# The sums of w34 begin in batch 0, in five operations for seven

## The chip, the cores and the metric

The kernel runs on one core of a Trainium2 chip. The metric is the device time of one execution in microseconds (us). Three runs of the kernel before took 485.19, 485.21 and 486.02 us, with a median of 485.21 us. The engines are TensorE (PE in the profile, PEld for its weight loads), VectorE (DVE), ScalarE (ACT), GpSimd (POOL) and SyncE (SP), which only issues transfers here.

## The reference

Shapes: x is (8, 8, 512, 64), state is (8, 8, 32, 64): eight batches, eight heads, 512 tokens, 32 states, width 64. The attention reads states for tokens and tokens for states with the same scores; its 544 rows for each batch then go through a bilinear layer and two linear maps.

```python
scores = scale * x @ state.T            # per batch and head
a  = softmax(scores, -1);    xread = a @ state
a2 = softmax(scores.T, -1);  sread = a2 @ x
X = concat([xread, sread], tokens)      # 8 * 544 rows of 512
out = ((X @ w1) * (X @ w2)) @ w3 @ w_out   # 512 -> 1024 -> 1024 -> 512
```

All is in float32; the kernel gets the weights as float64 bits and turns them into float32 itself.

## The kernel before

**What is computed in which form.** w3 @ w_out doesn't depend on the tokens. The kernel computes it once, in a prologue, as w34 (1024 x 512). For the products with a second operand split in two, each float32 value is held as a rounded part "hi" and a remainder "lo" (`split`: ACT writes hi, DVE subtracts to get lo), and a product is the sum of hi*hi, hi*lo and lo*hi. w34 stands so in the tiles `wo["hi"]` and `wo["lo"]`, which are eight row tiles of 128 (index FT), each with two halves of 256 columns.

**Batch 0.** For each of eight feature tiles `stage1(0, ft)` sums the two projections in a PSUM pair, and `hidden` multiplies the two and splits the result. Four "quarters" of two feature tiles each go by; `early_stage2(q)` adds the products of quarter q with `wo` for the first two of four token tiles, and is written one quarter later. `side_steps()` holds work for batch 1 (its scores, its softmax, the read of states) that is dealt out between them. After the quarters, a loop over the four token tiles tt does the rest of stage 2 (`stage2`), stores, runs a piece of side work and, for tt 0 to 2, calls `combine_weights(tt)`.

**Batches 1 to 7** go through `quarter_batch(b)`. It multiplies by w34 in a scheme of seven products for a 2 x 2 split of the product, with tokens and output columns in halves. Three of the products use blocks of w34 as they are (`b_part`), four use sums of blocks (`t_part`), which stand in the tile `t_both`, index j from 0 to 3, for each of the four k (QF is 4). `combine_weights(k)` fills the slot k. With b11, b12 the two column halves of row tile k, and b21, b22 those of row tile 4 + k, the four sums are

- t0 = b12 - b11
- t1 = b22 - t0
- t2 = b22 - b12
- t3 = b21 - t1

It adds hi and lo back together for the two row tiles (L412, twice, into two tiles named tmp), takes the four differences (L419, four times) in a tile `late` g_x, and splits them into `t_both` (L102 on ACT, L103 on DVE). The same g_x tile is later the place of the stage-1 results of token columns `x` in each `quarter_batch`, with a single buffer. The call for k = 3 stands in `quarter_batch` of batch 1 (`b == PLAIN`).

In `quarter_batch` the order on PE is: four pairs of feature tiles of stage 1 (`stage1_pair`, L438), then the products a11 (into `bank_a`), s3 (`bank_e`), a12, a22; then the read of states and the sets `sw` for the batch behind it (L268, L152); then the products s2, s1 and s4. `take` copies one half of a product out of PSUM on ACT (L477) and adds the other on DVE (L464); m1, m7, c11 and c21 are the tiles it fills. `quarter(src)` makes a split half tile (a11, a12, a22, s1 to s4).

**Softmax steps.** `scores()` is a generator. For b of 2 and more its steps are: the scores and their copy (L193); maxima, transposes and exponentials (L200 to L224); `token_order`, a block transpose on DVE (L229) and 16 block moves issued on SP (L177); the sums and the division (L238 to L244); the transpose of the weights (L249); their split. `next(softmax)` takes one step. The read of states ends with a transpose into `turned` (L278) and, for odd batches, another 16 block moves to `sread`.

**What sets the order.** PE and SP follow the program's order. ACT and DVE do so only in the prologue (until `order.close()`); after it a planner orders their instructions by the program's order as priority, by estimated durations and by when operands are there; `high_priority` lifts some of them. On the chip each engine takes its list in order. `issue_after(ins)` puts the instructions of a block behind `ins` on the engine of `ins`; `behind(two)` does so for an ACT and a DVE instruction together.

**Memory.** The prologue's pool `pro` holds the raw weights and conversion tiles. Its last use is the conversion of the second half of w1 and w2, at the end of quarter 0. The pool `late`, with `t_both` and its g_x tile, is opened when `pro` is closed and takes its place.

Of the kernel before, what the change touches and what calls it, by code (L numbers as in the profile page):

```python
# [22 lines left out]
F32 = mybir.dt.float32  # L23
F32R = mybir.dt.float32r
# [5 lines left out]
P = 128  # L30
# [9 lines left out]
def attn_bilinear_kernel(  # L40
# [140 lines left out]
    def attention_steps(b):  # L181
# [3 lines left out]
        def scores():  # L185
# [132 lines left out]
    last_split, stored, last_unit = [], [], []  # L318
# [89 lines left out]
    def combine_weights(k):  # L408

        raw = [tmp_tile() for _ in range(2)]  # L410
        for i, whole in enumerate(raw):
            nc.vector.tensor_tensor(  # L412
                out=by_halves(whole), in0=wo["hi"][:, i * QF + k].bitcast(F32), in1=wo["lo"][:, i * QF + k].bitcast(F32),
                op=ALU.add,
            )
        b11, b12, b21, b22 = (whole[:, half * HO:(half + 1) * HO] for whole in raw for half in range(2))
        t = whole_tile(late, F32)[:, :, :HO]
        for j, (x, y) in enumerate(((b12, b11), (b22, t[:, 0]), (b22, b12), (b21, t[:, 1]))):
            nc.vector.tensor_tensor(out=t[:, j], in0=x, in1=y, op=ALU.subtract)  # L419
        return split(t_both[:, :, k, 0], t_both[:, :, k, 1], t)  # L420
# [38 lines left out]
    def quarter_batch(b):  # L459
# [44 lines left out]
        first_pair = stage1_pair(b, 0, raw)  # L504
# [30 lines left out]
        with behind(take(m1, bank_a)):  # L535
# [51 lines left out]
    with tc.tile_pool(name="pro", bufs=2) as pro:  # L587

        places = [w_sb[:, n // 2, n % 2].rearrange("p j f -> p (j f)") for n in range(2 * QT)]
        w_out = [places[(FT + k) // 2][:, k % 2 * DO:(k % 2 + 1) * DO] for k in range(FT)]  # L590

        chunks = [places[k % (FT // 2)] for k in range(FT)]
        w3s, w34_ps = {}, {}

        def finish(i):
            split(wo["hi"][:, i], wo["lo"][:, i], by_halves(w34_ps[i][:, :DO]))

        def convert_first(k):
            ends = PARTS.get(k, (NW,))
            return to_f32(pro, w34_k[k], chunks[k], ends, (), wout=w_out[k])  # L600

        def w34_first(k):

            for i in range(FT // 2):
                nc.tensor.matmul(  # L605
                    w34_ps[i][:, :DO], chunks[k][:, DO + i * P:DO + (i + 1) * P], w_out[k],
                    start=(k == 0), stop=(k == FT - 1),
                )

        def convert_w3(i):  # L610
            w3s[i] = pro.tile([P, NW], F32, name="w3", bufs=2)
            return to_f32(pro, w3t[i - FT // 2], w3s[i])

        def w34(i, ks=range(FT)):
            if ks[0] == 0:
                w34_ps[i] = bank()
            for k in ks:
                nc.tensor.matmul(  # L618
                    w34_ps[i][:, :DO], w3s[i][:, k * P:(k + 1) * P], w_out[k], start=(k == 0), stop=(k == FT - 1)
                )  # L620

        def convert_half(n):

            return to_f32(pro, w12[n], places[n])

        def sets(quarter):
            for i in range(2):
                sw_quarter(0, quarter, i)


        gs, acc, early = [], [], range(2)

        def early_stage2(quarter):
            for tt in early:
                if quarter == 0:
                    acc.append(bank())
                for ft in range(2 * quarter, 2 * quarter + 2):
                    project(acc[tt], gs, tt, ft)

        order = ctx.enter_context(ExitStack())  # L640
        order.enter_context(tc.manual_schedule(engines={mybir.EngineType.Activation, mybir.EngineType.DVE}))
        pair = two_banks()
        w34_ps.update(enumerate([bank(), bank(), pair[:, 0], pair[:, 1]]))
        for k in range(FT + AHEAD):
            run([partial(convert_first, k) if k < FT else partial(convert_w3, k - FT // 2)])
            if k >= AHEAD:
                w34_first(k - AHEAD)
        load_x(0)
        scores, reads[0], _ = attention_steps(0)
        softmax = scores()  # L650
        next(softmax)
        finish(0)
        finish(1)
        for_two = pair[:, :, :DO].rearrange("p i (h o) -> p i h o", h=2)
        split(wo["hi"][:, 2:4], wo["lo"][:, 2:4], for_two)
        w34(4)

        w1_0, w2_0, w1_1, w2_1 = map(convert_half, range(4))
        go = lambda steps: next(steps, None)
        w3_6 = convert_w3(6)  # L660
        go(w1_0), go(softmax), go(w1_0)
        finish(4)
        go(w2_0), go(w3_6), go(softmax), go(w3_6)
        w34(5)
        go(softmax)
        go(w2_0)
        finish(5)
        w3_7 = convert_w3(7)
        go(w3_7), go(w3_7), go(w1_1), go(w1_1), go(w2_1), go(w2_1)
        load_tokens(0)  # L670
        w34(6)
        sets(0)
        finish(6)
        w34(7, range(LAST))
        sets(1)
        w34(7, range(LAST, FT))
        finish(7)
        order.close()
        for quarter in range(QT):
            stage1(0, 2 * quarter, gs)  # L680
            if quarter == 1:
                run(sw_steps(0)[2:])
            if quarter:
                early_stage2(quarter - 1)
            if quarter == 1:
                side = side_steps()
            elif quarter == 2:
                run(side.pop(0))
            stage1(0, 2 * quarter + 1, gs)
            if quarter == 0:  # L690
                run([partial(convert_half, n) for n in range(4, 2 * QT)])
                load_x(1)
                with tc.issue_after(last_split[1].ins):
                    go(softmax)
        run(side.pop(0))
        early_stage2(QT - 1)
# [3 lines left out]
    for tt in range(NT):  # L700
# [6 lines left out]
        if tt + 1 < QF:  # L707
            combine_weights(tt)
# [81 lines left out]
```

## Time and profile before

| | |
|---|---|
| runs | 485.19, 485.21, 486.02 us; median 485.21 |
| profiled execution | 485.49 us |
| its span, first to last instruction | 483.7 us |
| PE busy | 476.4 us (98%) |
| DVE busy | 398.6 us (82%) |
| ACT busy | 237.2 us (49%) |
| mean granted TensorE clock | 1.000 |

The page of the profile shows one execution. Times are microseconds from the start of the span, unless marked ns. L412 is line 412 of the kernel. A group's line gives line, engine, operation, the tiles written and read, the shapes, the count, the busy time and the mean ns of one. A timeline's line gives start, length, engine, line, operation, tiles, shapes and count of merged instructions, and in brackets the idle time before it and what ended it. An engine starts an instruction that depends on nothing recent some hundredths of a us before the one ahead of it ends, so starts count for sums and not lengths. A stage's line gives its length and then each engine's busy time with the number of instructions.

### The profile page before, as it was taken

Reading aid. Unit: us, or ns where it says so; the run is one execution under the profiler, and the core shown is the slowest. Engines: PE = TensorE matmul, PEld = TensorE weight load, DVE = VectorE, ACT = ScalarE, POOL = GpSimd, SP = SyncE. Lnnn points to the kernel's source line nnn. Section 1 sums busy time; section 2 is a strip of 40 time slices with the busy share of each in tenths; the row PEclk is TensorE's granted clock in tenths of the full one; section 3 lists DMA queues with packets and bytes.
Section 4 is the critical chain, followed back from the end, with each engine's and each line's share of the span. In section 5 each row is a group of like instructions: output and inputs, shape, how many; then the busy total and the mean of one; then the engine's idle time right before and its main releaser. Section 6 shows DMA issues by size and latency. Waiting matters only on the chain.

```text
span 483.7 us, 7886 instructions
## 1 busy us (share of the span) xinstructions
PE 476.4 (98%) x3166; PEld 359.2 (74%) x3166; DVE 398.6 (82%) x499; ACT 237.2 (49%) x300; POOL 0.2 (0%) x4
## 2 busy tenths in 40 slices
PE   8999999999999999999999999999999999999996
PEld 6444457777788588868877887888688878888885
DVE  5669897699799996999699969987998796569970
ACT  4777785353455533543363446254624470335640
POOL 0000000000000000000000000000000000000000
PEclk9999999999999999999999999999999999999999
DMA  8996991332621522052215212521311102001101
GB/s 341 362 360 257 360 328 24 114 121 64 210 49 29 186 70 41 22 207 58 37 34 193 55 32 81 172 46 25 110 68 25 19 26 74 1 0 45 45 1 43
DMA packets 55332, 52.42 MB, mean 108 GB/s; under 512 B 41728, under 2 KB 49920, under 8 KB 50688
## 3 DMA queue, kind: packets, MB, share of 16 engines
q1 hardware_dynamic: 46464, 43.27, 27.4%
q10 hardware_dynamic: 8832, 8.65, 5.2%
q8 instruction: 25, 0.41, 0.3%
q14 instruction: 11, 0.09, 0.1%
HBM read 38.27 MB, written 8.91 MB: 98 GB/s over the span
## 4 chain that ended last, share of the span: by engine, by line
PE 77%; DVE 9%; SPq 5%; ACT 3%; DMA 3%; issue 1%; DVEq 0%
PE ps L438 28%; PE ps L454 15%; PE ps_a L454 11%; SPq L177 5%; PE ps L152 4%; PE ps_o L371 3%; PE ps L728 3%; PE ps_o L605 3%; PE ps L605 3%; PE ps L371 2%; PE ps L729 2%; DMA raw<-in_w_dram 2%; PE ps L268 1%; ACT ulps L131 1%; ACT w_sb L123 1%; DVE g_lo L103 1%
## 5 line engine op out<-in xcount | busy, mean ns | idle before, releaser
L438 PE MATMUL ps<-at_lo,sw_hi 128*128 128x512 f32 x224 | 87.3, 390 | 0.0
L438 PE MATMUL ps<-at_hi,sw_hi 128*128 128x512 f32 x224 | 87.2, 389 | 0.0
L438 PE MATMUL ps<-at_hi,sw_lo 128*128 128x512 f32 x224 | 87.1, 389 | 0.0
L102 ACT CAST g_hi<-g_x 128x1024 fp32r<-128x1024 f32 x49 | 50.8, 1052 | 54.1 <-DVE g_x L446 42.1
L103 DVE TENSOR_TENSOR g_lo<-g_x,g_hi 128x1024 fp32r<-128x1024 f32 x49 | 59.2, 1219 | 9.3 <-ACT g_hi L102 9.3
L444 ACT COPY g_x<-ps 128x1024 f32<-128x1024 f32 x28 | 28.4, 1013 | 76.9 <-PE ps L438 64.8
L446 DVE TENSOR_TENSOR g_x<-g_x,ps 128x1024 f32<-128x1024 f32 x28 | 34.1, 1218 | 29.0 <-PE ps L438 28.9
L438 PEld LDWEIGHTS ps<-at_hi,sw_lo 128*128 128x128 f32 x224 | 42.0, 188 | 8.8
L438 PEld LDWEIGHTS ps<-at_lo,sw_hi 128*128 128x128 f32 x224 | 42.1, 188 | 8.7
L438 PEld LDWEIGHTS ps<-at_hi,sw_hi 128*128 128x128 f32 x224 | 42.1, 188 | 8.4
L454 PE MATMUL ps<-t,g_hi 128*128 128x512 f32 x168 | 42.1, 393 | 0.0
L464 DVE TENSOR_TENSOR g_x<-g_x 128x1024 f32<-128x1024 f32 x28 | 34.2, 1220 | 0.4
L454 PEld LDWEIGHTS ps<-t,g_hi 128*128 128x128 f32 x168 | 30.2, 189 | 5.4
L103 DVE TENSOR_TENSOR sw_lo<-ps,sw_hi 128x1024 fp32r<-128x1024 f32 (+1 forms) x28 | 30.5, 1135 | 0.2 <-ACT sw_hi L102 0.2
L464 DVE TENSOR_TENSOR tmp<-tmp,ps 128x512 f32<-128x512 f32 x42 | 28.7, 683 | 1.7
L618 PE MATMUL ps_o<-w_sb,w 128*128 128x512 f32 x64 | 28.5, 598 | 0.1
L454 PE MATMUL ps_a<-wo,g_hi 128*128 128x512 f32 x112 | 28.0, 392 | 0.4 <-DVE tmp L464 0.4
L102 ACT CAST sw_hi<-ps 128x1024 fp32r<-128x1024 f32 (+1 forms) x28 | 25.2, 970 | 0.6 <-PE ps L152 0.5
L152 PE MATMUL ps<-w_sb,st 64*32 64x512 f32 (+1 forms) x448 | 25.0, 561 | 0.2 <-DVE scaled L273 0.2
L123 ACT ACTIVATE w_sb<-raw 128x1024 f32<-128x1024 f32 (+3 forms) x18 | 18.7, 1052 | 11.3 <-DMA raw<-in_w_k_dram 9.4
L454 PEld LDWEIGHTS ps<-t,g_lo 128*128 128x128 f32 x168 | 22.9, 190 | 1.6
L454 PEld LDWEIGHTS ps_a<-wo,g_hi 128*128 128x128 f32 x112 | 20.6, 188 | 4.6 <-DVE tmp L464 0.6
(120 smaller groups left out, 796.5 us busy)
## 6 DMA issues: line engine op xcount, KB each, us to landing
raw<-in_w_k_dram SPq DMA_DIRECT2D x8, 1024.0 KB, 6.7
x_d<-in_x_d_dram SPq DMA_DIRECT2D x8, 1024.0 KB, 5.1
raw<-in_w_dram SPq DMA_DIRECT2D x8, 1024.0 KB, 6.6
x_s<-in_x_s_dram SPq DMA_DIRECT2D x8, 1024.0 KB, 5.7
out_dram<-tmp ACTq DMA_DIRECT2D x56, 128.0 KB, 1.7
raw<-in_w3t_dram SPq DMA_DIRECT2D x4, 1024.0 KB, 7.4
e<-work SPq DMA_DIRECT2D x112, 32.0 KB, 1.9
out_dram<-tmp ACTq DMA_DIRECT2D x4, 256.0 KB, 2.1
```

Source lines behind the costliest of these rows:

```text
L102: nc.scalar.copy(out=hi, in_=src),
L103: nc.vector.tensor_tensor(out=lo, in0=src, in1=hi.bitcast(F32), op=ALU.subtract),
L152: nc.tensor.matmul(ps[j * NS:(j + 1) * NS, q], sts[b][rows, j], moving(rows, j), start=True, stop=True)
L177: nc.sync.dma_start(out=dest(slice(c * NS, (c + 1) * NS), j), in_=src(slice(j * NS, (j + 1) * NS), c))
L371: nc.tensor.matmul(by_halves(ps[:, :DO]), g, wo[w][:, ft], start=(ft == 0 and k == 0), stop=(ft == FT - 1 and k == 2))
L438: nc.tensor.matmul(ps[:, kk], w[:, kt, cols], a[:, kt], start=(k == 0), stop=(k == 3 * KT - 1))
L444: nc.scalar.copy(out=mine, in_=ps)
L446: return nc.vector.tensor_tensor(out=mine, in0=mine, in1=ps, op=ALU.mult)
L454: nc.tensor.matmul(ps[:, tt, 1] if n else ps[:, tt], part, weights[:, 0] if n else weights, start=(fresh and k == 0 and n == 0), stop=(k = ...
L464: combine = lambda out, x, y, op: nc.vector.tensor_tensor(out=out, in0=x, in1=y, op=op)
L605: nc.tensor.matmul(w34_ps[i][:, :DO], chunks[k][:, DO + i * P:DO + (i + 1) * P], w_out[k], start=(k == 0), stop=(k == FT - 1),)
L618: nc.tensor.matmul(w34_ps[i][:, :DO], w3s[i][:, k * P:(k + 1) * P], w_out[k], start=(k == 0), stop=(k == FT - 1))
```

## The change

`combine_weights` is called for k = 0 in batch 0, behind its fourth feature tile (quarter 1, after `stage1(0, 3)`), with its DVE instructions behind batch 0's block transpose (`last_turn`, L229). The loop over the token tiles then calls it for k = 1, 2 and 3, so that none is left for batch 1. For that the pool `pro` is closed at the end of quarter 0 already, and `late` and `t_both` stand there.

A call has five operations on DVE in place of seven: one addition of hi and lo for both row tiles (1024 elements in each partition), one subtraction of 512 for t0 and t2, one of 256 each for t1 and t3, and the split's. Sums and differences stand side by side in the g_x tile of `late`; no tmp tile is used.

In batch 1 the softmax's division is no longer ordered behind the split of the k = 3 sums, and the transpose of the weights (L249) is ordered behind m1's sum, where it was behind m7's.

```diff
             def token_order():
                 blocks = work_tile()
-                nc.vector.transpose(out=flat(blocks), in_=flat(e2))
+                last_turn[:] = [nc.vector.transpose(out=flat(blocks), in_=flat(e2))]
...
     def combine_weights(k):
 
-        raw = [tmp_tile() for _ in range(2)]
-        for i, whole in enumerate(raw):
-            nc.vector.tensor_tensor(
-                out=by_halves(whole), in0=wo["hi"][:, i * QF + k].bitcast(F32), in1=wo["lo"][:, i * QF + k].bitcast(F32),
-                op=ALU.add,
-            )
-        b11, b12, b21, b22 = (whole[:, half * HO:(half + 1) * HO] for whole in raw for half in range(2))
-        t = whole_tile(late, F32)[:, :, :HO]
-        for j, (x, y) in enumerate(((b12, b11), (b22, t[:, 0]), (b22, b12), (b21, t[:, 1]))):
-            nc.vector.tensor_tensor(out=t[:, j], in0=x, in1=y, op=ALU.subtract)
-        return split(t_both[:, :, k, 0], t_both[:, :, k, 1], t)
+        x = whole_tile(late, F32)
+        t, raw = x[:, :, :HO], x[:, :, HO:]
+        combine = partial(nc.vector.tensor_tensor, op=ALU.subtract)
+        nc.vector.tensor_tensor(
+            out=raw.rearrange("p (i h) o -> p i h o", i=2),
+            in0=wo["hi"][:, k::QF].bitcast(F32), in1=wo["lo"][:, k::QF].bitcast(F32), op=ALU.add,
+        )
+        combine(out=t[:, ::2], in0=raw[:, 1::2], in1=raw[:, :2])
+        combine(out=t[:, 1], in0=raw[:, 3], in1=t[:, 0])
+        combine(out=t[:, 3], in0=raw[:, 2], in1=t[:, 1])
+        split(t_both[:, :, k, 0], t_both[:, :, k, 1], t)
...
-        first_pair = stage1_pair(b, 0, raw)
+        stage1_pair(b, 0, raw)
...
         next(softmax, None)
         if b == PLAIN:
             next(first_moves, None)
-            with tc.issue_after(first_pair.ins):
-                combined = combine_weights(QF - 1)
-            with behind(combined):
-                next(softmax)
-        else:
-            next(softmax, None)
+        next(softmax, None)
         stage1_pair(b, 1, raw)
...
         a12 = quarter(x[:, :, first])
-        with behind(take(m1, bank_a)):
+        took = take(m1, bank_a)
+        if b == PLAIN:
+            with behind(took):
+                next(softmax)
+        with behind(took):
             a22 = quarter(x[:, :, second])
...
         product(bank_e, s3, t_part(2), True)
-        took = take(m7, bank_e)
-        if b == PLAIN:
-            with behind(took):
-                next(softmax)
+        take(m7, bank_e)
...
             if quarter == 0:
                 run([partial(convert_half, n) for n in range(4, 2 * QT)])
                 load_x(1)
                 with tc.issue_after(last_split[1].ins):
                     go(softmax)
+                pro_pool.close()
+                late = ctx.enter_context(tc.tile_pool(name="late", bufs=1))
+                t_both = late.tile([P, 4, QF, 2, HO], F32R, name="t")
+            elif quarter == 1:
+                with tc.issue_after(last_turn[0].ins):
+                    combine_weights(0)
         run(side.pop(0))
         early_stage2(QT - 1)
-    late = ctx.enter_context(tc.tile_pool(name="late", bufs=1))
-    t_both = late.tile([P, 4, QF, 2, HO], F32R, name="t")
...
         run(side[tt])
         if tt + 1 < QF:
-            combine_weights(tt)
+            combine_weights(tt + 1)
```

The prologue's block is also indented one level less, since its pool is no longer closed by a `with`; nothing else in it changes.

More of the change, by code (lines that the diff above doesn't have):

```diff
@@ L315, in sw_quarter @@
         split(*(t[:, :, c * NQ:(c + 1) * NQ] for t in tiles[half, i]), ps)
-    last_split, stored, last_unit = [], [], []
+    last_split, stored, last_unit, last_turn = [], [], [], []
     QF = FT // 2
@@ L584, in run @@
                 pass
[L587 to L689, printed above, removed]
-            if quarter == 0:
[L691 to L696, printed above, removed]
@@ new lines, in convert_first, with w34_first, convert_w3 @@
+    def convert_first(k):
+        ends = PARTS.get(k, (NW,))
+        return to_f32(pro, w34_k[k], chunks[k], ends, (), wout=w_out[k])
+    def w34_first(k):
+        for i in range(FT // 2):
+            nc.tensor.matmul(
+                w34_ps[i][:, :DO], chunks[k][:, DO + i * P:DO + (i + 1) * P], w_out[k],
+                start=(k == 0), stop=(k == FT - 1),
+            )
+    def convert_w3(i):
+        w3s[i] = pro.tile([P, NW], F32, name="w3", bufs=2)
+        return to_f32(pro, w3t[i - FT // 2], w3s[i])
@@ new lines, in w34, with convert_half, sets, early_stage2 @@
+    def w34(i, ks=range(FT)):
+        if ks[0] == 0:
+            w34_ps[i] = bank()
+        for k in ks:
+            nc.tensor.matmul(
+                w34_ps[i][:, :DO], w3s[i][:, k * P:(k + 1) * P], w_out[k], start=(k == 0), stop=(k == FT - 1)
+            )
+    def convert_half(n):
+        return to_f32(pro, w12[n], places[n])
+    def sets(quarter):
+        for i in range(2):
+            sw_quarter(0, quarter, i)
+    gs, acc, early = [], [], range(2)
+    def early_stage2(quarter):
+        for tt in early:
+            if quarter == 0:
+                acc.append(bank())
+            for ft in range(2 * quarter, 2 * quarter + 2):
+                project(acc[tt], gs, tt, ft)
@@ new lines, in attn_bilinear_kernel @@
+    order = ctx.enter_context(ExitStack())
+    order.enter_context(tc.manual_schedule(engines={mybir.EngineType.Activation, mybir.EngineType.DVE}))
+    pair = two_banks()
+    w34_ps.update(enumerate([bank(), bank(), pair[:, 0], pair[:, 1]]))
+    for k in range(FT + AHEAD):
+        run([partial(convert_first, k) if k < FT else partial(convert_w3, k - FT // 2)])
+        if k >= AHEAD:
+            w34_first(k - AHEAD)
+    load_x(0)
+    scores, reads[0], _ = attention_steps(0)
+    softmax = scores()
@@ new lines, in attn_bilinear_kernel @@
+    next(softmax)
+    finish(0)
+    finish(1)
+    for_two = pair[:, :, :DO].rearrange("p i (h o) -> p i h o", h=2)
+    split(wo["hi"][:, 2:4], wo["lo"][:, 2:4], for_two)
+    w34(4)
+    w1_0, w2_0, w1_1, w2_1 = map(convert_half, range(4))
+    go = lambda steps: next(steps, None)
+    w3_6 = convert_w3(6)
+    go(w1_0), go(softmax), go(w1_0)
+    finish(4)
+    go(w2_0), go(w3_6), go(softmax), go(w3_6)
+    w34(5)
+    go(softmax)
+    go(w2_0)
+    finish(5)
+    w3_7 = convert_w3(7)
+    go(w3_7), go(w3_7), go(w1_1), go(w1_1), go(w2_1), go(w2_1)
@@ new lines, in attn_bilinear_kernel @@
+    load_tokens(0)
+    w34(6)
+    sets(0)
+    finish(6)
+    w34(7, range(LAST))
+    sets(1)
+    w34(7, range(LAST, FT))
+    finish(7)
+    order.close()
+    for quarter in range(QT):
+        stage1(0, 2 * quarter, gs)
+        if quarter == 1:
+            run(sw_steps(0)[2:])
+        if quarter:
+            early_stage2(quarter - 1)
+        if quarter == 1:
+            side = side_steps()
+        elif quarter == 2:
+            run(side.pop(0))
+        stage1(0, 2 * quarter + 1, gs)
+        if quarter == 0:
+            run([partial(convert_half, n) for n in range(4, 2 * QT)])
+            load_x(1)
+            with tc.issue_after(last_split[1].ins):
+                go(softmax)
+            pro_pool.close()
[4 more added lines that the diff above has]
+                combine_weights(0)
@@ L700, in attn_bilinear_kernel @@
+    run(side.pop(0))
+    early_stage2(QT - 1)
     for tt in range(NT):
```

8 lines of the change are left out of this document (added).

## The prediction

> **What bounds the kernel now.** I read the page's busy times, then what TensorE (PE) waited for, then busy time by stage, and last the order of VectorE's (DVE) instructions around each wait.
>
> ```profile
> span 483.7 us, 7886 instructions
> ...
> PE 476.4 (98%) x3166; PEld 359.2 (74%) x3166; DVE 398.6 (82%) x499; ACT 237.2 (49%) x300; POOL 0.2 (0%) x4
> ```
> ```profile
> PE ps_a L454 <- DVE sw_lo L103: 0.5, 1, 0.5
> PE ps_a L454 <- DVE tmp L464: 0.4, 1, 0.4
> PE ps L152 <- DVE scaled L273: 0.2, 1, 0.2
> PE ps_o L371 <- DVE g_lo L103: 0.2, 1, 0.2
> ```
>
> PE is busy for 98% of the span, and the change touches no matmul. So it can only earn what PE loses by waiting. Apart from two waits at the start, these four are all of it, each of them for DVE. Next, the second part of batch 1 (products, and the sets for the batch behind it) beside the same part of batch 2:
>
> ```profile
> 143.80:170.81 27.01, 25.85 (x257) 19.47 (x256) 25.65 (x29) 13.24 (x16) 0.00 (x0) 1.00 0.33 108
> 192.60:217.81 25.21, 25.21 (x257) 19.60 (x256) 23.95 (x27) 12.81 (x15) 0.00 (x0) 1.00 0.32 110
> ```
>
> The columns are length, then busy time of PE, weight load, DVE, ACT, POOL, then clock and DMA. Both have the same 257 matmuls: 27.01 us in batch 1, 25.21 in batch 2, where PE never waits. The difference, **1.80 us, is the most that relief in batch 1 can earn**; three of the four waits lie there. The idle time is less than that, because a stall also slows the matmuls after it.
>
> ```profile
> 143.80 1.98 PE L454 MATMUL ps_a<-wo,g_hi 128*128 128x512 f32 x8
> ...
> 146.57 2.00 PE L454 MATMUL ps<-t,g_hi 128*128 128x512 f32 x8
> ...
> 149.94 2.14 PE L454 MATMUL ps_a<-wo,g_hi 128*128 128x512 f32 x8 [0.41 <-DVE tmp L464]
> ...
> 159.86 1.95 PE L152 MATMUL ps<-w_sb,st 64*32 64x512 f32 x32 [0.24 <-DVE scaled L273]
> 162.32 2.11 PE L454 MATMUL ps_a<-t,g_hi 128*128 128x512 f32 x8 [0.51 <-DVE sw_lo L103]
> ```
>
> DVE is 25.65 of 27.01 us busy in that part: it arrives late and stays late. The sums of w34 for the last k (L412, L419, the t split at L103) are in the queue that makes it late:
>
> ```profile
> 126.62 1.29 DVE L412 TENSOR_TENSOR tmp<-wo 128x512 f32<-128x512 f32 x2
> 127.82 0.75 DVE L419 TENSOR_TENSOR g_x<-tmp 128x256 f32<-128x256 f32 x2
> 128.49 1.21 DVE L200 TENSOR_REDUCE m<-work 128x2 f32<-128x1024 f32 x1
> ...
> 135.96 0.88 DVE L419 TENSOR_TENSOR g_x<-tmp,g_x 128x256 f32<-128x256 f32 x2
> 137.16 1.23 DVE L103 TENSOR_TENSOR g_lo<-g_x,g_hi 128x1024 fp32r<-128x1024 f32 x1 [0.32 <-ACT g_hi L102]
> 138.30 1.22 DVE L103 TENSOR_TENSOR t<-g_x,t 128x1024 fp32r<-128x1024 f32 x1
> 139.43 0.16 DVE L238 TENSOR_SCALAR sum<-sum 128x2 f32<-128x2 f32 x1
> ...
> 145.73 1.22 DVE L446 TENSOR_TENSOR g_x<-g_x,ps 128x1024 f32<-128x1024 f32 x1
> 148.06 1.22 DVE L103 TENSOR_TENSOR g_lo<-g_x,g_hi 128x1024 fp32r<-128x1024 f32 x1 [1.11 <-ACT g_hi L102]
> 149.20 0.68 DVE L464 TENSOR_TENSOR tmp<-tmp,ps_a 128x512 f32<-128x512 f32 x1
> ...
> 152.07 0.68 DVE L464 TENSOR_TENSOR tmp<-tmp,ps 128x512 f32<-128x512 f32 x1
> ...
> 153.80 1.23 DVE L249 STREAM_TRANSPOSE work<-work 128x1024 f32<-128x1024 f32 x1
> ...
> 161.09 1.18 DVE L103 TENSOR_TENSOR sw_lo<-ps_a,sw_hi 128x1024 fp32r<-128x1024 f32 x1
> ```
>
> **The change, part by part.** *First, the last sums leave batch 1.* By starts, L412 and the first L419 pair hold DVE from 126.62 to 128.49, 1.87 us; the second pair 0.88; the t split from 138.30 to 139.43, 1.13. Together 3.88. Not all of it can be used. L200 reads ACT's copy of the scores:
>
> ```profile
> 126.50 1.01 ACT L193 COPY work<-ps 128x1024 f32<-128x1024 f32 x1 [1.99 <-PE ps L152]
> ...
> 139.60 1.01 ACT L444 COPY g_x<-ps 128x1024 f32<-128x1024 f32 x1 [1.53 <-DVE sum L238]
> ```
>
> It ends at 127.51, so L200 moves from 128.49 to about 127.55 and 0.93 of the 3.88 goes idle, leaving 2.95. (The second row is a side gain: that copy writes the tile in which the sums stood, and started when the t split at 138.30 ended. It need not wait any more.) Next cap: L446 at 145.73 multiplies the last stage-1 sums, and cannot run before PE has them. In batch 2:
>
> ```profile
> 192.60 1.75 PE L454 MATMUL ps_a<-wo,g_hi 128*128 128x512 f32 x7
> ```
> ```profile
> 192.87 1.22 DVE L446 TENSOR_TENSOR g_x<-g_x,ps 128x1024 f32<-128x1024 f32 x1 [3.08 <-PE ps L438]
> ```
>
> There it starts 0.27 behind the first product, which in batch 1 is 143.80 + 0.27 = 144.07. So of the 2.95 only 145.73 - 144.07 = **1.66 us** is usable from here on, and the other 1.29 becomes idle time. Behind it DVE has its old list, in which nothing else waits for PE: the split at 148.06 waits for ACT, which waits for L446. All starts 1.66 earlier. The sum at 149.20 frees its bank in time for the third product at 143.80 + 2 x 2.77 = 149.34 (a product takes 146.57 - 143.80 = 2.77 us), and the sw_lo split moves from 161.09 to 159.43. PE then resumes at 162.32 - 1.66 = 160.66, where batch 2's pace would bring it at 162.32 - 1.80 = 160.52. The gain is 1.66, with 0.14 still waited.
>
> *Second, the transpose at L249 moves* from behind m7's sum (152.07) to behind m1's (149.20). It keeps its place ahead of everything after 153.80, so nothing later changes. What is now queued behind it is the a22 split, which followed the sum at 149.20, and m7's sum; each loses 1.14 of its 1.66. The split starts near 149.20 + 0.60 - 1.66 + 1.14 = 149.3 and ends at 150.5; m7's sum ends at 152.07 + 0.60 - 1.66 + 1.14 = 152.15 at the latest. PE wants both for the fourth product, a22's, at 149.34 + 2.77 = 152.11. I cost it at nothing; bounds 0 and 1.14, the transpose itself. Its work buffer is freed by the block moves on SP:
>
> ```profile
> 133.83 10.39 SPq L177 DMA_DIRECT2D e<-work  x16
> ```
>
> They follow L229, which also moves up, so they land by 146.1 (144.22 and about 1.9), before 148.1. No DMA is added, and SP's list keeps its order.
>
> *Third, the sums for k = 0 are put into batch 0,* behind its block transpose, so from about 78 on. Nearest rows for an operation (mean ns in the first fence; shortest, median and longest ns, first and last start in the second):
>
> ```profile
> L464 DVE TENSOR_TENSOR g_x<-g_x 128x1024 f32<-128x1024 f32 x28 | 34.2, 1220 | 0.4
> ...
> L419 DVE TENSOR_TENSOR g_x<-tmp 128x256 f32<-128x256 f32 x8 | 3.0, 417 | 0.0
> ```
> ```profile
> L412 DVE TENSOR_TENSOR tmp<-wo x8: 647/682/684, 106.8 to 127.2; 128x512 f32<-128x512 f32 x8
> ```
>
> One addition of 1024 (1.22), one subtraction of 512 (0.68), two of 256 (0.42 each), the split (1.22, as at 138.30): 3.96 us of DVE, and one ACT pass over 1024 (1.0, as L193). The wide addition reads four runs of 256; L464 does so too. The room:
>
> ```profile
> 77.90:90.52 12.62, 12.62 (x68) 9.53 (x67) 6.46 (x10) 4.87 (x7) 0.00 (x0) 1.00 0.27 44
> 90.52:96.45 5.93, 5.76 (x26) 4.42 (x24) 5.90 (x8) 2.41 (x6) 0.00 (x0) 1.00 0.53 186
> 104.50:125.50 21.00, 21.00 (x123) 15.80 (x129) 18.22 (x29) 9.98 (x12) 0.00 (x0) 1.00 0.39 115
> ```
> ```profile
> 85.04 0.69 DVE L103 TENSOR_TENSOR g_lo<-tmp,g_hi 128x512 fp32r<-128x512 f32 x1 [0.69 <-ACT g_hi L102]
> 90.52 1.25 DVE L205 STREAM_TRANSPOSE work<-ps 128x1024 f32<-128x1024 f32 x1 [2.01 <-DMA work<-work]
> ```
> ```profile
> 86.70 0.39 PE L371 MATMUL ps_o<-wo,g_lo 128*128 128x512 f32 x1
> ```
>
> From 77.90 to 90.52 DVE is idle for 12.62 - 6.46 = 6.16 us and ACT for 7.75, so the cover holds: cost nothing. Without it: the fourth tile's split ends at 85.73 and PE reads it at 86.70, a slack of 0.97. One wide operation ahead of it (1.22) makes PE wait 0.25, an ACT pass beside it 1.25. Some 0.2 of that comes back: PE is idle for 5.93 - 5.76 = 0.17 at the end of the next stretch, for a chain that starts with the DMA at 90.52. Bounds 0 and 1.25; a gain is excluded, because nothing is taken out of this stretch.
>
> *Fourth, the end of batch 0* has k = 1 to 3 in five operations each, for k = 0 to 2 in seven. PE is busy for all of 104.50 to 125.50, so a few tenths on DVE are worth nothing there. But one tile now holds all of a k, so the next addition waits for the split before: three times 3.96 + 1.0 from the start of the present ones, near 106.8, end at 121.7, ahead of 126.62.
>
> [...]
>
> *The sum:* 485.49 us (the profiled execution: span 483.7 and 1.79 around it) - 1.66 + 0 + 0 + 0 = 483.83. The median, 485.21, lies 0.28 below that execution, so the forecast is **483.55 us**.
>
> **The rivals.** A difference under 0.2% (0.97 us) can't be told from none here.
>
> *The relief is eaten by the new order (15%).* The order on DVE and ACT is planned, and in-order: if L249 or a softmax step comes ahead of m7's sum at the wrong time, PE waits up to 1.14 at the a22 product. For it: the slack of nothing computed above. Against it: m7's product ends at 149.34, so its sum could come 2 us earlier than this latest place. The same loss twice, at m7 and at the sw_lo split, takes all. Time: 483.55 + 1.14 = 484.7, up to no change, 485.2.
>
> *Batch 0 costs a part (10%).* An operation stands in front of the fourth tile's split: 0.25 to 1.25. Time 483.8 to 484.8; for it, the slack of 0.97 is less than one wide operation; against it, the idle gaps.
>
> *Slower (10%).* The new sums fall behind 90.52, on the softmax chain of batch 1, which PE already waits for at 96.45. DVE is idle there only for hundredths, so each us put there is a us of PE: all of it costs 3.96, and 483.55 + 3.96 = 487.5. It decides from 1.66 us on, which is the wide addition with one subtraction. For it: the order is planned from estimated times, which can differ from the chip's. Against it: the sums need nothing that isn't there by 78, and stand ahead of that chain in the program.
>
> *The sums still reach into batch 1:* the t split of k = 3 ends behind 126.62 if the serial chain stretches by 5 us. Then the first 0.93, which is idle anyway, goes first and the gain stays above 1; it is within the first case.
>
> **How the numbers follow.** The forecast's case has 65%, with its own range 482.9 (all 1.80, the 0.2 of 96.45 and a few tenths for the run) to 484.2. Adding the rivals, 482.9 to 485.4 leaves out the slower case and little else. Faster by more than 0.97: 65% and half of the batch-0 case, 70%. Same: most of the eaten case and the other half, 19%. Slower: 11%.
>
> **What would show it.** Right: batch 1's first matmul of L454 to batch 2's first of L438 takes 25.2 to 25.5 us for 27.01; the waits for tmp, scaled and sw_lo shrink or go; L446 starts 0.3 behind the first product; DVE is busier between 78 and 90; the wait at 96.45 stays near 0.2. Wrong: any new wait of PE between 78 and 97, DVE work on the new sums behind 90.5, or a wait of the a22 product for m7's sum.

## The result and the profile after

The kernel after the change took a median of 488.29 us (486.94 to 489.23, six runs), and the kernel before, beside it, 485.20 us (485.13 to 486.02, six runs). The ratio is 1.0057 with a 95% interval of 1.0047 to 1.0066: slower by 0.57%, about 2.8 us (the two medians lie 3.09 apart). The forecast was 483.55 us, in a range up to 485.4 us. The profiled execution took 488.12 us with a span of 486.3 us, 2.6 us more than the 483.7 us of before.

The page's span and busy times, after:

```profile
span 486.3 us, 7881 instructions
...
PE 477.0 (98%) x3166; PEld 359.4 (74%) x3166; DVE 397.6 (82%) x491; ACT 236.9 (49%) x300; POOL 0.2 (0%) x4
```

DVE has eight instructions fewer (499 to 491: two for each of the four k), so the change does what it says. Next, busy time by stage: batch 0 from its first stage-1 matmul of the feature tiles (L357) to batch 1's first (L438), and the second part of batch 1, from its first product (L454) to batch 2's first L438. The part between them took 24.04 us for 24.03. The columns are length, busy time of PE, weight load, DVE, ACT and POOL, then clock and DMA. First both stages of after, then batch 0 of before:

```profile
66.76:123.98 57.22, 54.76 (x370) 39.15 (x369) 50.70 (x68) 28.53 (x41) 0.00 (x0) 0.97 0.31 97
148.02:173.46 25.44, 25.27 (x257) 19.61 (x256) 23.81 (x27) 12.81 (x15) 0.00 (x0) 1.00 0.35 114
```
```profile
66.72:119.77 53.05, 52.88 (x371) 38.41 (x369) 45.25 (x64) 26.76 (x38) 0.00 (x0) 1.00 0.35 107
```

The second part of batch 1 takes 25.44 us for 27.01: of the forecast gain of 1.66 us, 1.57 is there. Batch 0 takes 57.22 us for 53.05 and loses 4.17. The balance, 4.17 - 1.57 = 2.60, is the whole difference of the spans. PE's waits after (the two at the start left out):

```profile
PE ps_o L371 <- ACT g_hi L102: 2.2, 1, 2.2
...
PE ps_o L371 <- DVE g_lo L103: 0.3, 1, 0.3
PE ps_a L454 <- DVE sw_lo L103: 0.2, 1, 0.2
```

Of the four waits of before only 0.2 us (sw_lo) is left, and a new wait of 2.2 + 0.3 us stands in batch 0. In PE's timeline after:

```profile
88.62 0.73 PE L371 MATMUL ps_o<-wo,g_hi 128*128 128x512 f32 x2 [2.18 <-ACT g_hi L102]
89.63 0.78 PE L371 MATMUL ps_o<-wo,g_lo 128*128 128x512 f32 x1 [0.28 <-DVE g_lo L103]
```

DVE's and ACT's timeline after, around this wait:

```profile
83.74 1.05 ACT L102 CAST t<-g_x 128x1024 fp32r<-128x1024 f32 x1 [3.00 <-DVE g_x L419]
84.70 0.58 ACT L326 COPY tmp<-ps 128x512 f32<-128x512 f32 x1
84.83 1.23 DVE L103 TENSOR_TENSOR t<-g_x,t 128x1024 fp32r<-128x1024 f32 x1 [1.17 <-ACT t L102]
86.09 1.23 DVE L413 TENSOR_TENSOR g_x<-wo 128x1024 f32<-128x1024 f32 x1
87.23 0.68 DVE L327 TENSOR_TENSOR tmp<-tmp,ps 128x512 f32<-128x512 f32 x1
87.94 0.62 ACT L102 CAST g_hi<-tmp 128x512 fp32r<-128x512 f32 x1 [2.67 <-DVE tmp L327]
...
93.07 1.23 DVE L413 TENSOR_TENSOR g_x<-wo 128x1024 f32<-128x1024 f32 x1
94.21 1.24 DVE L205 STREAM_TRANSPOSE work<-ps 128x1024 f32<-128x1024 f32 x1
```

The same copy and product of the fourth feature tile before:

```profile
83.05 0.59 ACT L326 COPY tmp<-ps 128x512 f32<-128x512 f32 x1 [2.01 <-PE ps L357]
83.67 0.69 DVE L327 TENSOR_TENSOR tmp<-tmp,ps 128x512 f32<-128x512 f32 x1 [1.16 <-ACT tmp L326]
```

Three instructions of the new sums stand ahead of the fourth tile. On ACT, the cast for k = 0 waits 3.00 us for its last subtraction (L419), and the copy L326 behind it starts at 84.70 for 83.05. On DVE, the split of k = 0 into `t` (84.83, called the t split here) stands ahead, and then the addition for **k = 1** (86.09), which the prediction had behind 106. L327 so starts at 87.23 for 83.67, 3.56 us later. The addition for k = 2 follows at 93.07, ahead of batch 1's softmax (L205 at 94.21).

The clock by stretches of 2 us, after (the column behind POOL is the granted clock):

```profile
88.00:90.00 2.00, 1.10 (x3) 0.67 (x4) 1.97 (x4) 1.05 (x2) 0.00 (x0) 0.92 0.30 49
90.00:92.00 2.00, 2.00 (x6) 1.52 (x6) 1.39 (x4) 1.57 (x2) 0.00 (x0) 0.50 0.15 33
92.00:94.00 2.00, 2.00 (x20) 0.50 (x18) 1.97 (x2) 0.00 (x0) 0.00 (x0) 0.73 0.00 0
```

Behind the wait the clock falls to half. Against a clock of 1.00, these three stretches lose 2 x (0.08 + 0.50 + 0.27) = 1.70 us. PE's idle time in batch 0 rises from 0.17 to 2.46 us (2.18 + 0.28), by 2.29, and its busy time from 52.88 to 54.76, by 1.88: together the 4.17 us. The clock makes 1.70 of the 1.88.

### The profile page after: what moved, and what is told of

Same layout as the page of the kernel before. It is cut to its first block, busy times and chain, and to the rows that moved or that the text cites. A ratio compares the mean times of both kernels' runs of the same rounds, so it can differ in the third digit from the quotient of the medians.

```text
span 486.3 us, 7881 instructions
## 1 busy us (share of the span) xinstructions
PE 477.0 (98%) x3166; PEld 359.4 (74%) x3166; DVE 397.6 (82%) x491; ACT 236.9 (49%) x300; POOL 0.2 (0%) x4
## 4 chain that ended last, share of the span: by engine, by line
PE 83%; DVE 10%; ACT 3%; DMA 2%; issue 1%; DVEq 0%; ACTq 0%
PE ps L438 31%; PE ps L454 15%; PE ps_a L454 11%; PE ps L152 5%; PE ps_o L371 4%; PE ps L728 3%; PE ps_o L602 3%; PE ps L602 3%; PE ps L371 2%; PE ps L357 2%; PE ps L729 2%; DVE g_lo L103 1%; PE ps L268 1%; DMA raw<-in_w_dram 1%; DVE w_sb L139 1%; DMA raw<-in_w_k_dram 1%
## 5 line engine op out<-in xcount | busy, mean ns | idle before, releaser
L438 PE MATMUL ps<-at_lo,sw_hi 128*128 128x512 f32 x224 | 87.3, 390 | 0.0
L438 PE MATMUL ps<-at_hi,sw_hi 128*128 128x512 f32 x224 | 87.2, 389 | 0.0
L438 PE MATMUL ps<-at_hi,sw_lo 128*128 128x512 f32 x224 | 87.1, 389 | 0.0
L446 DVE TENSOR_TENSOR g_x<-g_x,ps 128x1024 f32<-128x1024 f32 x28 | 34.1, 1216 | 35.8 <-PE ps L438 35.8
L438 PEld LDWEIGHTS ps<-at_hi,sw_lo 128*128 128x128 f32 x224 | 42.1, 188 | 8.8
L438 PEld LDWEIGHTS ps<-at_lo,sw_hi 128*128 128x128 f32 x224 | 42.1, 188 | 8.7
L438 PEld LDWEIGHTS ps<-at_hi,sw_hi 128*128 128x128 f32 x224 | 42.1, 188 | 8.4
L454 PE MATMUL ps<-t,g_hi 128*128 128x512 f32 x168 | 42.1, 392 | 0.0
L454 PEld LDWEIGHTS ps<-t,g_hi 128*128 128x128 f32 x168 | 30.2, 189 | 5.4
L454 PE MATMUL ps_a<-wo,g_hi 128*128 128x512 f32 x112 | 27.9, 391 | 0.0
L454 PEld LDWEIGHTS ps<-t,g_lo 128*128 128x128 f32 x168 | 22.9, 190 | 1.6
L615 PEld LDWEIGHTS ps_o<-w_sb,w 128*128 128x128 f32 x64 | 11.8, 190 | 16.0 <-issue 14.6
L454 PEld LDWEIGHTS ps_a<-wo,g_hi 128*128 128x128 f32 x112 | 20.6, 188 | 4.0
```

The source lines that it names most:

```text
L438: nc.tensor.matmul(ps[:, kk], w[:, kt, cols], a[:, kt], start=(k == 0), stop=(k == 3 * KT - 1))
L446: return nc.vector.tensor_tensor(out=mine, in0=mine, in1=ps, op=ALU.mult)
L454: nc.tensor.matmul(ps[:, tt, 1] if n else ps[:, tt], part, weights[:, 0] if n else weights, start=(fresh and k == 0 and n == 0), stop=(k = ...
L615: nc.tensor.matmul(w34_ps[i][:, :DO], w3s[i][:, k * P:(k + 1) * P], w_out[k], start=(k == 0), stop=(k == FT - 1))
```

## The experiments

Two questions had to be told apart: what brought the sums of k = 1 and 2 so far forward, and how much of the loss is theirs and how much comes from k = 0, the one that was meant to be here. A third was whether the place of L249 matters. Each experiment's ratio is to the kernel before on the same chip, whose median beside them was 485.55 to 485.60 us. Stages are read from one profiled execution of each kernel.

**The form of the sums alone: e3_five.** The kernel before, with the five operations in the body of `combine_weights`; its calls, for k = 0 to 2 in the token loop and k = 3 in batch 1, stay.

```diff
-        raw = [tmp_tile() for _ in range(2)]
...
+        x = whole_tile(late, F32)
+        t, raw = x[:, :, :HO], x[:, :, HO:]
...
+            out=raw.rearrange("p (i h) o -> p i h o", i=2),
+            in0=wo["hi"][:, k::QF].bitcast(F32), in1=wo["lo"][:, k::QF].bitcast(F32), op=ALU.add,
```

> The kernel before with nothing changed but the form of the sums: five operations in one g_x tile for seven with two tmp tiles; k = 0 to 2 in the token loop and k = 3 in batch 1, the pool opened where it was. Theory A (the tmp tiles held the sums back): the planner runs k = 0 to 2 into the stretch from 74 to 98 us though they stand in the token loop, PE waits there for 1.5 us or more, the time goes to 487 to 489.5. Rival D (the early pool, or the call behind the fourth tile, is what lets them run ahead): PE's list of waits as before, 484.9 to 485.6.

Measured: 490.29 us (489.66 to 491.09), ratio 1.0096 (1.0082 to 1.0110). Its batch 0, then its additions on DVE:

```profile
66.76:123.96 57.20, 53.98 (x370) 37.93 (x369) 46.97 (x63) 27.71 (x40) 0.00 (x0) 1.00 0.33 102
```
```profile
74.48 1.22 DVE L413 TENSOR_TENSOR g_x<-wo 128x1024 f32<-128x1024 f32 x1
85.79 1.23 DVE L413 TENSOR_TENSOR g_x<-wo 128x1024 f32<-128x1024 f32 x1
92.48 1.22 DVE L413 TENSOR_TENSOR g_x<-wo 128x1024 f32<-128x1024 f32 x1
```

The sums that the program calls in the token loop ran at 74 to 92 us, where before they began at 106.8. Without the new call and without the earlier pool the form alone loses 57.20 - 53.05 = 4.15 us in batch 0, as much as the whole change, and gains nothing in the second part of batch 1 (27.00 for 27.01). The time came out 0.8 us above the range expected for theory A, 487 to 489.5; the order that it expected is there.

**Is it the number of operations, or the tile? e10_seven_own.** The kernel before with its seven operations, whose two additions write the second half of the k's own g_x tile in place of two tmp tiles.

```diff
-        raw = [tmp_tile() for _ in range(2)]
+        x = whole_tile(late, F32)
+        raw = [x[:, :, HO:].rearrange("p (i h) o -> p i h o", i=2)[:, i] for i in range(2)]
...
-        t = whole_tile(late, F32)[:, :, :HO]
+        t = x[:, :, :HO]
```

> The kernel before with one thing changed: the two additions of each k write the second half of the k's own whole tile, in place of two tiles of the tmp pool. Seven operations stay seven, and nothing else moves. Theory T (the tmp tiles held the sums back in the token loop): the sums of k = 0 to 2 now run ahead into the stretch from 74 to 105 us, as with five operations; L327 of the fourth tile starts after 85 for 83.67, PE waits over 1 us in all between 78 and 105, batch 0 takes 55 to 57.5 us for 53.05, and the time is 487.5 to 490.5. Rival N (the number or the lengths of the operations made the planner run them ahead, not the tiles): the first addition stays behind 104 as before, and the time is 485.2 to 485.7.

Measured: 489.81 us (489.53 to 490.01), ratio 1.0086 (1.0072 to 1.0100). Batch 0, and the additions:

```profile
66.94:124.32 57.38, 53.96 (x371) 38.06 (x369) 47.13 (x69) 27.42 (x40) 0.00 (x0) 1.00 0.32 98
```
```profile
75.44 1.29 DVE L413 TENSOR_TENSOR g_x<-wo 128x512 f32<-128x512 f32 x2
...
86.88 1.29 DVE L413 TENSOR_TENSOR g_x<-wo 128x512 f32<-128x512 f32 x2
88.10 0.68 DVE L327 TENSOR_TENSOR tmp<-tmp,ps 128x512 f32<-128x512 f32 x1
...
93.58 1.29 DVE L413 TENSOR_TENSOR g_x<-wo 128x512 f32<-128x512 f32 x2
```

The count and lengths of the operations are those of before; only where the additions write is different, and they run ahead by 31 us (75.44 for 106.81). Theory T came true in the time, in batch 0 and in the late L327. So **the tmp tiles held the sums in the token loop**. The feature tiles' copies (L326, L327) use the same pool of four; that a tile of it is given out in the order of the program, so that the sums get theirs only behind the copies issued ahead of them, is read from the code and was not tested by itself.

**The whole change, with tmp tiles again: e5_tmp.** The kernel after with the old body of `combine_weights` (the body's change in the diff of e3_five, the other way round), all calls where the change puts them.

> The changed kernel with the seven-operation form of the sums, its two additions written to tmp tiles as in the kernel before; places as in the change. Theory A in its narrower form (what held the sums back before was the four tmp buffers that they share with the feature tiles' products, and the five-operation form needs none): k = 1 to 3 stay in the token loop, the cast for k = 0 lands behind the fourth tile's, PE loses 0 to 0.6 us between 78 and 97, time 483.5 to 484.3. Rival D (the pool that is opened early lets them run ahead): as the changed kernel, 487 to 488.5.

Measured: 484.12 us (483.65 to 484.51), ratio 0.9968 (0.9956 to 0.9981). Batch 0 and the second part of batch 1, then the cast for k = 0 and its surroundings:

```profile
67.31:120.33 53.02, 52.90 (x371) 38.40 (x369) 48.81 (x71) 27.96 (x40) 0.00 (x0) 1.00 0.33 107
144.39:169.84 25.45, 25.27 (x257) 19.60 (x256) 23.82 (x27) 12.81 (x15) 0.00 (x0) 1.00 0.34 113
```
```profile
83.66 0.59 ACT L326 COPY tmp<-ps 128x512 f32<-128x512 f32 x1 [2.28 <-PE ps L357]
84.28 0.69 DVE L327 TENSOR_TENSOR tmp<-tmp,ps 128x512 f32<-128x512 f32 x1 [0.83 <-ACT tmp L326]
...
88.33 1.04 ACT L102 CAST t<-g_x 128x1024 fp32r<-128x1024 f32 x1
...
107.31 1.27 DVE L412 TENSOR_TENSOR tmp<-wo 128x512 f32<-128x512 f32 x2
```

k = 1 to 3 are in the token loop again (from 107.31), the cast for k = 0 comes behind the fourth tile's copy, and batch 0 costs nothing: 53.02 us. The gain in batch 1 stays. The earlier end of `pro` is in this kernel too, so it isn't what cost the time.

**Only k = 0 in batch 0, in the new form: e1_hold.** The kernel after, with k = 1 to 3 held in the token loop behind the split of the last feature tile (`last_split` has the last split's two instructions, on ACT and DVE).

```diff
-            combine_weights(tt + 1)
+            with tc.issue_after(last_split[1].ins):
+                combine_weights(tt + 1)
```

> The changed kernel with the sums for k = 1 to 3 held, on DVE, behind the split of batch 0's last feature tile; only k = 0 stays behind the fourth. Theory A (the loss is the sums of k = 1 and later, which the planner ran ahead into the stretch from 86 us on): without them L327 of the fourth tile starts some 1.2 us earlier, PE waits about 1 us in place of 2.2 and no TensorE clock below 1.00 follows, so about 484.7 us. Rival B (k = 0 alone does the harm, by its cast standing ahead of the fourth tile's copy on ACT and its split ahead of L327 on DVE): PE's wait stays at 2 us or more and the time at 487 to 488.5.

Measured: 485.96 us (484.92 to 486.79), ratio 1.0008 (0.9999 to 1.0017). Batch 0; then the order on ACT; on DVE; then PE:

```profile
66.78:121.33 54.55, 53.11 (x370) 38.33 (x369) 48.57 (x64) 28.52 (x41) 0.00 (x0) 1.00 0.33 102
```
```profile
84.29 1.05 ACT L102 CAST t<-g_x 128x1024 fp32r<-128x1024 f32 x1 [3.00 <-DVE g_x L419]
85.25 0.58 ACT L326 COPY tmp<-ps 128x512 f32<-128x512 f32 x1
```
```profile
85.38 1.23 DVE L103 TENSOR_TENSOR t<-g_x,t 128x1024 fp32r<-128x1024 f32 x1 [1.18 <-ACT t L102]
86.52 0.68 DVE L327 TENSOR_TENSOR tmp<-tmp,ps 128x512 f32<-128x512 f32 x1
```
```profile
87.90 0.74 PE L371 MATMUL ps_o<-wo,g_hi 128*128 128x512 f32 x2 [1.44 <-ACT g_hi L102]
```

Batch 0 loses 54.55 - 53.05 = 1.50 us for 4.17, and the clock stays at 1.00. So k = 1 and 2 running ahead make 57.22 - 54.55 = 2.67 us of the loss, the clock's 1.70 among them. The rest is k = 0 itself: the wide addition for k = 1 is gone; the cast ahead of L326 and the t split ahead of L327 are not. The wait and the clock are near what theory A expected. The time isn't, 485.96 us for about 484.7: batch 0 loses 1.50 us, and batch 1's second part took 26.26 us in this run (last section).

**The cast for k = 0 behind the fourth tile: e8_cast.** As e1_hold, and the split of k = 0, its cast on ACT and its t split on DVE, is held behind the fourth tile's split.

```diff
+        with ExitStack() as held:
+            for ins in hold:
+                held.enter_context(tc.issue_after(ins))
+            split(t_both[:, :, k, 0], t_both[:, :, k, 1], t)
...
-                combine_weights(0)
+                combine_weights(0, [two.ins for two in last_split])
```

> As the kernel with k = 1 to 3 held behind the last feature tile, and k = 0 early, but the split of the k = 0 sums (its ACT cast and its last DVE operation) is held behind the fourth tile's split; its addition and subtractions stay where they were. Theory G (what PE waits for at 87.9 us is the cast that stands in ACT's list ahead of the fourth tile's copy and waits for the subtractions): the wait of 1.4 us goes, batch 0 is 1.3 to 1.6 us shorter, time 484.0 to 484.7. Rival H (the addition and subtractions on DVE delay the fourth tile by themselves, or the split held back delays the softmax chain from 90.5 on): a wait of 0.6 us or more stays, at 86 to 88 or at 96.

Measured: 484.43 us (483.53 to 484.89), ratio 0.9975 (0.9963 to 0.9986).

```profile
66.77:119.36 52.59, 52.59 (x371) 38.40 (x370) 48.47 (x64) 28.03 (x40) 0.00 (x0) 1.00 0.33 104
```
```profile
83.09 0.59 ACT L326 COPY tmp<-ps 128x512 f32<-128x512 f32 x1 [2.33 <-PE ps L357]
84.97 1.05 ACT L102 CAST t<-g_x 128x1024 fp32r<-128x1024 f32 x1
```

PE is busy for all of batch 0 (52.59 of 52.59 us). This profile is of the kernel's fastest run (483.53 us); e11_cast_m7 below, which differs only in L249 and was profiled at its median, has 53.16 us, still 1.39 less than e1_hold. So the wait of 1.44 us came from the place of this split: on ACT a cast that waits for DVE, in front of a copy that PE needs, and on DVE the t split in front of the product. The experiment moves both. In e1_hold's rows the copy ended at 85.25 + 0.58 = 85.83 and L327 began at 86.52, behind the t split, so about 0.7 us of the delay is DVE's order and the rest ACT's; no run takes them apart.

**All four sums late: e2_late, and L249 as before: e7_late_m7.** The kernel after without the call in quarter 1; the token loop has k = 0 and 1, then 2, then 3, held as in e1_hold. e7_late_m7 is the same with L249 behind m7's sum again.

```diff
-        elif quarter == 1:
-            with tc.issue_after(last_turn[0].ins):
-                combine_weights(0)
...
+            with tc.issue_after(last_split[1].ins):
+                for k in ((0, 1), (2,), (3,))[tt]:
+                    combine_weights(k)
```

> The changed kernel with all four k behind the split of batch 0's last feature tile (k = 0 and 1 for the first token tile, then 2 and 3); nothing is put behind the fourth feature tile. Theory A: PE's list between 78 and 97 is as in the kernel before, the gain in batch 1 (27.01 to 25.4 us for its second part) stays, so 483.5 us (483.1 to 484.0). Rival C (four calls are too much for DVE from 104 to 126 us, the last split ends behind batch 1's first products of stage 1 and batch 1 is late again): second part of batch 1 at 26 us or more, time 484.3 to 485.2.

> The kernel with all four k held in the token loop, and the transpose L249 of batch 1 behind m7's sum again, as in the kernel before. My step (moving L249 is worth nothing): within 0.3 us of the kernel that differs from it only in L249. Rival E (the move is a good part of batch 1's gain): 0.8 us slower than that, or more.

Measured: 484.50 us (483.57 to 485.33), ratio 0.9977 (0.9968 to 0.9986), and 483.97 us (483.48 to 485.02), ratio 0.9966 (0.9956 to 0.9976). The second part of batch 1, first e2_late and then e7_late_m7:

```profile
144.17:170.39 26.22, 25.27 (x257) 19.60 (x256) 24.38 (x28) 12.81 (x15) 0.00 (x0) 1.00 0.36 114
```
```profile
143.69:169.12 25.43, 25.28 (x258) 19.61 (x256) 24.07 (x28) 12.81 (x15) 0.00 (x0) 1.00 0.38 118
```

All four k have room without a loss, so nothing had to go behind the fourth tile: batch 0 took 53.19 and 52.80 us. They don't all end in it. In e7_late_m7 batch 1 begins at 119.63, the addition for k = 3 starts at 124.16 and its t split at 128.15, and the second part still takes 25.43 us. So sums that end some 10 us earlier than before (138.30, t split of k = 3) cost nothing in batch 1. e2_late met the numbers of rival C (26 us or more, 484.3 to 485.2), but e7_late_m7 has the same four calls at the same places without the loss, so the four calls aren't its cause. e7_late_m7 missed both of its expectations: it is 0.53 us below e2_late in the median, neither within 0.3 nor slower. The 0.8 us between the two profiles is more than the 0.02 that L249 is worth in the next experiment; in e2_late an output store's issue held ACT (last section).

**L249 alone: e4_m1.** The kernel before, with the division and transpose steps of the softmax behind m1's sum.

```diff
-        with behind(take(m1, bank_a)):
+        took = take(m1, bank_a)
+        if b == PLAIN:
+            with behind(took):
+                next(softmax)
+        with behind(took):
...
-        took = take(m7, bank_e)
-        if b == PLAIN:
-            with behind(took):
-                next(softmax)
+        take(m7, bank_e)
```

> The kernel before with only the transpose L249 of batch 1 moved, from behind m7's sum to behind m1's. My step (worth nothing): within 0.4 us of the kernel before. Rival F (the move costs by itself, as the pair of runs with the sums held late hints with 0.8 us in batch 1's second part): second part of batch 1 at 27.5 us or more, 485.9 to 486.5.

Measured: 485.37 us (485.13 to 486.29), ratio 0.9997 (0.9988 to 1.0006).

```profile
143.57:170.56 26.99, 25.61 (x258) 19.62 (x256) 25.63 (x29) 13.11 (x16) 0.00 (x0) 1.00 0.34 108
```

26.99 us for 27.01: worth nothing by itself. This kernel also shows how far two profiles of one stage can differ: the edit doesn't touch batch 0, which took 52.75 us here and 53.05 in the profile of before. So differences of 0.3 us in batch 0 are read as none.

**The versions that beat both: e9_tmp_m7 and e11_cast_m7.** e5_tmp and e8_cast, each with L249 behind m7's sum as before the change (the diff of e4_m1 the other way round).

> The change with the sums in the seven-operation form with tmp tiles, and L249 of batch 1 behind m7's sum as in the kernel before. What is left of the change is that the sums for k = 0 start behind batch 0's fourth feature tile and none is left for batch 1. If my first step (the relief in batch 1, 1.66 us) holds without the move of L249: 483.4 to 484.2, no more than 0.4 us from the same kernel with L249 behind m1.

> The kernel with the split of k = 0 held behind the fourth tile's split (which took 484.43), and with L249 behind m7's sum as before the change. Theory M (the place of L249 is worth nothing): 484.2 to 484.7, the second part of batch 1 25.4 to 25.5 us. Rival (behind m1 it costs up to 0.5 us, as the medians of the two kernels with all sums late would have it): 483.6 to 484.1, with the gain in the stretch behind the third product of batch 1.

Measured: 483.70 us (483.51 to 483.89), ratio 0.9960 (0.9947 to 0.9972), and 484.07 us (483.57 to 484.38), ratio 0.9964 (0.9953 to 0.9976). e9_tmp_m7 by stages:

```profile
67.07:119.70 52.63, 52.63 (x371) 38.40 (x369) 48.81 (x71) 27.64 (x39) 0.00 (x0) 1.00 0.34 104
...
143.76:169.18 25.42, 25.27 (x258) 19.61 (x256) 23.79 (x27) 12.82 (x15) 0.00 (x0) 1.00 0.35 113
```

PE waits nowhere in batch 0. With L249 behind m7 the median of each of three pairs came out lower, by 0.53, 0.42 and 0.36 us (e7_late_m7 to e2_late, e9_tmp_m7 to e5_tmp, e11_cast_m7 to e8_cast). Every pair's intervals overlap, and in the last two the profiles show only 0.03 and 0.04 us of it in the second part (25.45 to 25.42, 25.46 to 25.42). Three equal signs speak for a small cost of the new place when the sums are gone; where the rest of it arises isn't settled. e9_tmp_m7 met its time and missed its distance to e5_tmp by 0.02 us (0.42 for at most 0.4). Both of e11_cast_m7's expectations are half right: its stage is the one's, its time the other's.

All stages side by side (us, each from its first matmul to the first of the next, in the profiled execution; medians of all runs; ratios to the kernel before on the same chip, so the medians of the rows compare only within some tenths):

| kernel | batch 0 | second part of batch 1 | median | ratio |
|---|---|---|---|---|
| before | 53.05 | 27.01 | 485.20 | |
| after | 57.22 | 25.44 | 488.29 | 1.0057 |
| e3_five | 57.20 | 27.00 | 490.29 | 1.0096 |
| e10_seven_own | 57.38 | 27.01 | 489.81 | 1.0086 |
| e1_hold | 54.55 | 26.26 | 485.96 | 1.0008 |
| e4_m1 | 52.75 | 26.99 | 485.37 | 0.9997 |
| e2_late | 53.19 | 26.22 | 484.50 | 0.9977 |
| e8_cast | 52.59 | 25.46 | 484.43 | 0.9975 |
| e5_tmp | 53.02 | 25.45 | 484.12 | 0.9968 |
| e11_cast_m7 | 53.16 | 25.42 | 484.07 | 0.9964 |
| e7_late_m7 | 52.80 | 25.43 | 483.97 | 0.9966 |
| e9_tmp_m7 | 52.63 | 25.42 | 483.70 | 0.9960 |

## Why the prediction was wrong

**First step, the relief in batch 1: right.** The second part was to take 25.2 to 25.5 us and took 25.44; L446 was to start 0.27 behind the first product, and the timeline after has it so (148.29 behind 148.02):

```profile
148.29 1.22 DVE L446 TENSOR_TENSOR g_x<-g_x,ps 128x1024 f32<-128x1024 f32 x1 [1.70 <-PE ps L438]
```

1.57 of the 1.66 us came, with 0.17 still waited (0.14 was forecast). e9_tmp_m7, where the rest of the change costs nothing, is 485.55 - 483.70 = 1.85 us below the kernel before. Its profile has 1.59 of that in the second part of batch 1 (27.01 - 25.42); the other tenths lie in batch 0, within the difference of two profiles.

**Second step, L249: right within its bounds** of 0 to 1.14. Alone it is worth 0.02 us of the stage (e4_m1); without the sums it may cost some 0.4 us. Neither decided anything.

**Third step, the sums for k = 0 behind the fourth tile: wrong, in the way that one of its rivals names.** It argued from idle time: DVE idle for 6.16 us and ACT for 7.75 between 77.90 and 90.52, "so the cover holds: cost nothing". Idle time of an engine is not room where the order on it is fixed. ACT was idle because it waited, and the cast for k = 0 took a place in its list ahead of the copy that PE needs; it made the copy wait for DVE's chain of subtractions, and the t split then stood ahead of the product on DVE. e1_hold gives k = 0's cost by itself, 1.50 us, at or above the bound of 1.25 (two profiles of this stage differ by 0.3). That bound had the lengths of the operations in it and not their waits. It is of the kind that the "batch 0 costs a part" rival names (an operation in front of the fourth tile's split); e8_cast takes these places in the lists away and with them the cost. The slack of 0.97 us that the prediction worked out was the right figure to look at; the prediction put the step at the lower bound, nothing, and the measured cost lies at the upper one or past it.

**Fourth step, the end of batch 0: this one failed with the larger loss.** It took it as given that k = 1 to 3 stay in the token loop: "three times 3.96 + 1.0 from the start of the present ones, near 106.8". That start was not a property of where the calls stand in the program but of the tmp tiles that the old form took, and the change took these away. The text of the change says that no tmp tile is used; the prediction counted what that saves in operations and not what the tiles had kept in place. In the profile of before, the sign was there: the last of w34's halves was written 35 us before the first addition, and that addition starts only behind the last product of a feature tile, which uses the same pool:

```profile
71.27 0.68 DVE L103 TENSOR_TENSOR wo<-ps_o,wo 128x512 fp32r<-128x512 f32 x1
...
101.81 0.69 DVE L327 TENSOR_TENSOR tmp<-tmp,ps 128x512 f32<-128x512 f32 x1 [0.18 <-ACT tmp L326]
...
106.81 1.27 DVE L412 TENSOR_TENSOR tmp<-wo 128x512 f32<-128x512 f32 x2
```

An operation that starts much later than its operands is held by something, and it has to be named before the start is used as a term. The result was 2.67 us of loss that had no term and no bound (e1_hold to after), 1.70 of them by the clock, which no term of the sum had either. The range, whose upper end was no change, didn't hold it. These 2.67 us are more than the whole gain of 1.57. The third step weighs too: e1_hold, which has its cost and not the fourth's, is no faster than the kernel before (ratio 1.0008), though 0.8 us of that lie in batch 1 (26.26 for 25.44).

**The rivals.** "Slower" had the right sign and a sum near the time (up to 487.5 us), but by another mechanism: it put the sums on the softmax chain behind 90.52. k = 2 did fall there (93.07, with L205 at 94.21 behind it), yet PE's wait of before at the end of that chain (96.45) is gone in the list after, since PE itself came late; all of PE's new idle time lies at the fourth tile (86 to 90 us). "The relief is eaten by the new order" did not happen.

## What to carry to other kernels

A shared buffer is also an order: before taking operations off a pool, ask which start times in the trace of before it was holding, and if the order is wanted, write it down (e8_cast) or keep the buffer (e5_tmp). Idle time of an in-order engine is room only at the places where its list doesn't wait; ask for each new instruction what stands right behind it and who waits for that. And an operation that waits for another engine costs more than its own length when it stands ahead of critical work: the copy L326 started at 83.05 in the kernel before and starts at 84.70 after; of the 1.65 us between them 0.69 is the cast's wait (it starts at 83.74) and 0.96 the cast.

## What the runs showed of the hardware

**A short stall can take the clock with it.** After the idle time of 2.18 and 0.28 us the granted clock of the profile after was 0.50 from 90 to 92 us. In e1_hold a wait of 1.44 us was followed by none of it (1.00 in every stretch of 2 us from 86 to 96), nor were e3_five's 1.82 + 0.28 us and e10_seven_own's 1.95 + 0.23 us in their profiles. The six runs of the kernel after had mean clocks of 0.995 to 0.999; the one with 0.999 was the fastest, 486.94 us. The Trainium skill, "TensorE: Matmul & The Clock Gate", section "What's actually happening", has the clock at half after an idle window of about 3.4 us, in windows that run freely. The half agrees with the 0.50; the idle time here was shorter than that, 2.46 us with two short matmuls in between, so by the measurement it is no safe limit for a stall. Why 2.46 us sufficed and 2.10 and 2.18 in the two others did not is open.

**With the clock at 1.00, a wait of PE still costs more than its idle time.** In e3_five PE was idle for 57.20 - 53.98 = 3.22 us of batch 0, and busy for 53.98 where before it was 52.88, 1.10 us more for the same work. Its rows have an explanation. Matmuls of 0.39 us that follow one another start 0.23 apart (85.43 and 85.66 in its timeline), so the last one ahead of a wait counts 0.16 us more as busy than it does in a row of them. The one behind a wait took 0.50, and the next started 0.34 behind it (89.33 and 89.67), 0.11 more. That makes an estimated 0.27 us for each wait. e3_five has five waits in batch 0 (1.82, 0.28, 0.52, 0.42 and 0.18 us) and the kernel before one (0.17): four more make about 1.1 us.

**A store's issue can hold ACT.** In e2_late, ACT's timeline has two output stores (L494) taking 1.73 us together, and the next copy out of PSUM behind them:

```profile
154.46 1.73 ACTq L494 DMA_DIRECT2D out_dram<-tmp  x2
156.29 0.59 ACT L477 COPY tmp<-ps 128x512 f32<-128x512 f32 x1 [1.32 <-DMA out_dram<-tmp]
```

In e9_tmp_m7 the same issues took 0.34 us each. e1_hold shows the long form as well, and both have the second part of batch 1 at 26.2 to 26.3 us in place of 25.4, with a wait of 0.9 to 1.0 us for sw_lo. No run takes the long issue away by itself, so that it makes the difference is argued from the rows. What makes the issue long wasn't found.
